# First loads in three DMAs, and three matmul units more beside the last division: one edit of a tuned attention and GLU kernel

## The chip, the cores and the metric

The kernel runs on one core of a Trainium2 chip. The metric is device time in microseconds (us) of one execution. TensorE is called PE in the profile (PEld is its weight load), VectorE DVE, ScalarE ACT, GpSimd POOL and SyncE SP. SP's queue issues most of the DMAs.

## The reference, cut to what matters

```python
x  = A_x                                   # [1, 2048, 512], bf16
xn = (x - mean(x)) / sqrt(var(x) + 1e-5)   # over the 512 columns
# A: 32 heads of 16, causal, window of 256 positions
q, k, v = split(xn @ wqkv)                 # wqkv [512, 1536]
p = softmax(where(0 <= i - j < 256, q @ k.T / 4, -1e9))
a = (p @ v) @ wo                           # wo [512, 512]
# B: gated bilinear layer, F = 1792
b = ((xn @ w_gate) * (xn @ w_up)) @ w_down
out = x + a + b
```

## The kernel before

The 2,048 rows are 16 blocks of 128, and four blocks make a chunk; there are four chunks (T = 0 to 3). All weights are loaded once and stay in SBUF. For each chunk the normalized rows are transposed (`xnT`), projected to Q, K and V (`proj_qk`, `proj_v`), scored, exponentiated and masked strip by strip (`scores`, `mask_diag`), multiplied with V (`values`), divided by the softmax sums (`divide`, which leaves `OT`), and projected with Wo. Beside it run the gate and up matmuls, whose product `hT` goes through Wd (`down`) into the same PSUM sums as the Wo product (`wo`). `store` adds x and writes a block out.

The program order is written out by hand; there is no automatic scheduler. `run` walks through the strips of scores and calls `fill`, which places waiting pieces of work from the list of `fillers` between them. Each piece has a cost in units of one matmul of 512 columns, and `fill(upto)` takes pieces in order as long as half a piece still fits. PSUM tiles come from a pool of four buffers (`ps_m`); behind the last scores the score tiles' four banks become `late[0]` to `late[3]`.

At the start, `setup` puts all loads on SP's queue, in order: blocks 0 and 1 of x, half of the V columns of Wqkv (rows 0 to 255), block 2, the other half, block 3, then the K and the Q columns, and after them the gate and up weights and the rest. PE meanwhile multiplies an identity matrix 38 times (L92). `first_chunk` then takes blocks 0 to 3 through statistics (`norm_stats`, DVE), `norm_scale` (1/sqrt, mostly POOL), `norm_apply` (DVE, gives `xn`), transposes on PE into a PSUM tile `xTp` (L187), a copy by ACT into `xnT` (L189), and the V projection (`vp`, L202). Block 0's four transposes go into one PSUM tile and are copied in two halves. DVE's order is statistics of block 0, of block 1, apply 0, statistics 2, apply 1, statistics 3, apply 2, apply 3. PE's order is transposes 0, transposes 1, V of block 0, transposes 2, V of 1, transposes 3, V of 2, V of 3, then the first K and Q projections (`qkp`, L214). In what follows V0 to V3 are these V projections.

At the end, once the last `values` is done, DVE transposes and divides (L324 to L338) and PE goes on with fillers: `fill(spent + 12)`. Ten matmuls of `down` for block 2 and three of `wo` for block 2 (the head groups 0 to 2) are placed there. Then come the last head group's `wo` for blocks 0 to 2 with their stores, the remaining fillers (`down` of block 3 in two column halves, since its sum is split between `late[3]` and a tile `psd3`), `add_x` for the second half, `wo` of block 3, and two stores: DVE and SP for the first half, ACT for the second.

Of the kernel before, what the change touches and what calls it, by code (L numbers as in the profile page):

```python
# [7 lines left out]
BF16 = mybir.dt.bfloat16  # L8
F32 = mybir.dt.float32
I32 = mybir.dt.int32  # L10
ACT = mybir.ActivationFunctionType
# [14 lines left out]
class Kernel:  # L26
# [26 lines left out]
    def setup(self):  # L53
        nc, const, NT, NF = self.nc, self.const, self.NT, self.NF
        self.x = const.tile([128, NT, 512], BF16, name="x")
        self.Wqkv = const.tile([128, 4, 1536], BF16, name="Wqkv")
        self.Wo = const.tile([128, 4, 512], BF16, name="Wo")
        self.Wg = const.tile([128, 4, self.F], BF16, name="Wg")
        self.Wu = const.tile([128, 4, self.F], BF16, name="Wu")
        self.Wd = const.tile([128, NF, 512], BF16, name="Wd")  # L60
        xv = self.x_d.rearrange("(t p) d -> p t d", p=128)
        wq = self.w_d["qkv"].rearrange("(k p) n -> p k n", p=128)
        wg = self.w_d["g"].rearrange("(k p) n -> p k n", p=128)
        wu = self.w_d["u"].rearrange("(k p) n -> p k n", p=128)
        for b in range(4):
            nc.sync.dma_start(out=self.x[:, b:b + 1, :], in_=xv[:, b:b + 1, :])
            if b in (1, 2):
                ks = slice(2 * b - 2, 2 * b)
                nc.sync.dma_start(out=self.Wqkv[:, ks, 1024:1536], in_=wq[:, ks, 1024:1536])
        for lo in (512, 0):  # L70
            nc.sync.dma_start(out=self.Wqkv[:, :, lo:lo + 512], in_=wq[:, :, lo:lo + 512])
        h = self.F // 2
        for lo in (0, h):
            nc.sync.dma_start(out=self.Wg[:, :, lo:lo + h], in_=wg[:, :, lo:lo + h])
            nc.sync.dma_start(out=self.Wu[:, :, lo:lo + h], in_=wu[:, :, lo:lo + h])
            if lo == 0:
                nc.sync.dma_start(out=self.x[:, 4:8, :], in_=xv[:, 4:8, :])
        nc.sync.dma_start(out=self.Wd[:], in_=self.w_d["d"].rearrange("(f p) n -> p f n", p=128))
        nc.sync.dma_start(out=self.Wo[:], in_=self.w_d["o"].rearrange("(c p) n -> p c n", p=128))
        nc.sync.dma_start(out=self.x[:, 8:NT, :], in_=xv[:, 8:NT, :])  # L80

        warm = const.tile([128, 1], F32, name="warm")
        nc.vector.memset(warm[:], 0.0)
        nc.scalar.activation(out=warm[:], in_=warm[:], func=ACT.Exp)
        ident = const.tile([128, 128], BF16, name="ident")
        nc.gpsimd.memset(ident[:], 0.0)
        nc.gpsimd.affine_select(out=ident[:], in_=ident[:], compare_op=ALU.not_equal, fill=1.0,
                                base=0, pattern=[[-1, 128]], channel_multiplier=1)
        self.ident = ident
        wps = self.ps_m.tile([128, 128], F32, tag="M", name="wps")  # L90
        for _ in range(38):
            nc.tensor.matmul(wps[:], lhsT=ident[:], rhs=ident[:], start=True, stop=True)  # L92
        pi = const.tile([128, 1], I32, name="pi")
        nc.gpsimd.iota(pi[:], pattern=[[0, 1]], base=0, channel_multiplier=1)
        podd = const.tile([128, 1], I32, name="podd")
        nc.vector.tensor_scalar(out=podd[:], in0=pi[:], scalar1=4, scalar2=1,
                                op0=ALU.arith_shift_right, op1=ALU.bitwise_and)
        self.odd = const.tile([128, 1], F32, name="odd")
        nc.vector.tensor_copy(out=self.odd[:], in_=podd[:])
        self.mhalf = const.tile([128, 4], F32, name="mhalf")  # L100
        nc.gpsimd.memset(self.mhalf[:], -0.5)
        self.diag = const.tile([128, 64], BF16, name="diag")
        self.far = const.tile([128, 64], BF16, name="far")
        nc.gpsimd.memset(self.diag[:], BIG)
        nc.gpsimd.memset(self.far[:], BIG)
        for half in (slice(0, 64), slice(64, 128)):
            self.triangle(self.diag[half], True)
            self.triangle(self.far[half], False)
        self.xnT, self.Q, self.hT, self.O, self.OT = {}, {}, {}, {}, {}
        self.K, self.Ko, self.V, self.VS = {}, {}, {}, {}  # L110
        self.strips, self.at = {}, {}
# [63 lines left out]
    def norm_transpose(self, t, by_dma):  # L175

        nc = self.nc
        xn = self.xns.pop(t)
        T, b = divmod(t, 4)
        if b == 0:  # L180
            self.xnT[T] = self.chunk2.tile([128, 4, 4, 128], BF16, tag="xnT", name=f"xnT{T}")
        if by_dma:
            nc.sync.dma_start_transpose(out=self.xnT[T][:, b, :, :], in_=xn[:])
            return
        ps = self.ps_m.tile([128, 4, 128], BF16, tag="M", name="xTp")
        for k in range(4):
            nc.tensor.transpose(ps[:, k, :], xn[:, 128 * k:128 * k + 128], self.ident[:])  # L187
        for ks in (slice(0, 2), slice(2, 4)) if b == 0 else (slice(0, 4),):
            nc.scalar.activation(out=self.xnT[T][:, b, ks, :], in_=ps[:, ks, :], func=ACT.Copy)  # L189

    def bank(self, ks, name):

# [174 lines left out]
    def down(self, T, b, lo, hi):  # L367

        nc = self.nc
        if lo == 0:  # L370
            if T == self.NCH - 1 and b == 3:
                last = self.ps_m.tile([128, 256], F32, tag="M", name="psd3")
                self.sums[b] = [(self.late[3][:, 0:256], 0, 256), (last[:], 256, 512)]
            elif T == self.NCH - 1 and b == 2:
                self.sums[b] = [(self.late[2][:], 0, 512)]
            else:
                self.sums[b] = [(self.ps_m.tile([128, 512], F32, tag="M", name="psd")[:], 0, 512)]
        for f in range(lo, hi):
            for ps, c0, c1 in self.sums[b]:
                nc.tensor.matmul(ps, lhsT=self.hT[T][:, f, 128 * b:128 * b + 128],  # L380
                                 rhs=self.Wd[:, f, c0:c1], start=(f == 0), stop=False)
# [26 lines left out]
    def fillers(self):  # L408
# [54 lines left out]
        for T in range(NCH):  # L463
            if T:
                if T + 1 < NCH:
                    for i, fs in norms(T + 1, 0, 1).items():
                        self.beside[self.first[T, 0] + (0, 2, 3, 4, 5)[i]] = fs
                down(T - 1, 0)
                wo(T - 1, 0, (0, 1))
                for b in range(4):  # L470
                    if b < 3:
                        down(T - 1, b + 1, range(0, NF - 2, 2))
                    wo(T - 1, b, (2, 3))
                    add(0, lambda T=T, b=b: self.store(T - 1, b))
                    if b < 3:
                        down(T - 1, b + 1, range(NF - 2, NF, 2))
                        wo(T - 1, b + 1, (0, 1))
            gu(T, norms(1, 1, 3) if T == 0 else {})
            if T + 1 < NCH:
                project(T + 1)  # L480
# [9 lines left out]
    def run(self):  # L490
# [18 lines left out]
        spent, n, scored = 0, 0, 0  # L509
        valued, ready = -1, -1  # L510

        def fill(upto, group):
            nonlocal spent, n
            while n < len(work):
                cost, f, before, after = work[n]
                if after is not None and after > valued:
                    break
                if spent + cost / 2 > upto and not any(
                        w[2] is not None and w[2] <= group for w in work[n:]):
                    break  # L520
                self.act_free = spent + cost - scored >= ACT_FREE
                f()
                spent += cost
                n += 1
# [29 lines left out]
        T = NCH - 1  # L554
# [7 lines left out]
        spent += VALUES  # L562
        divide(len(steps) - 1)
        valued = ready
        fill(spent + 12, -1)
        for b in range(3):
            self.wo(T, b, (3,))
            self.store(T, b, on_act=(b == 1))
# [42 lines left out]
```

## Time and profile before

| | us |
|---|---|
| median of 4 runs | 270.5 |
| lowest and highest run | 270.32, 271.99 |
| profiled execution, whole | 271.99 |
| its span, first to last instruction | 270.3 |
| PE busy in the span | 260.0 (96%) |
| DVE busy | 181.5 (67%) |
| ACT busy | 170.8 (63%) |
| POOL busy | 113.6 (42%) |

Busy PE time is modelled from pipelined matmuls whose records overlap by their latency, so it is an upper bound of PE's own work. The share of an engine is an average over the span; the prediction reads it by stretch. The profile also shows the clock that TensorE was granted, as a share of its full clock: 0.994 on average over this span.

### The profile page before, as it was taken

To read this page: it belongs to the slowest core of one execution; us is meant where nothing else is said; L and a number is where in the kernel's file an instruction comes from. 1 tells how busy PE (TensorE), PEld (TensorE's weight loads), DVE (VectorE), ACT (ScalarE), POOL (GpSimd) and SP (SyncE) were. 2 spreads that over 40 slices of the span, in tenths; PEclk is the share of its full clock that TensorE was granted. 3 is DMA by queue.
4 is the path that set the end of the run, shared out by engine and by line. 5 is a ranking of instruction groups with operands and counts; after the bars stand their busy time and mean duration, and the time that the engine had idled before them with its cause. 6 is when DMAs were issued, how large, how long until landed. Compare 5 with 4: busy or idle time off the path is not lost.

```text
span 270.3 us, 8862 instructions
## 1 busy us (share of the span) xinstructions
PE 260.0 (96%) x3860; PEld 120.8 (45%) x3882; DVE 181.5 (67%) x352; ACT 170.8 (63%) x132; POOL 113.6 (42%) x281
## 2 busy tenths in 40 slices
PE   7799999999999999999999999999999999999994
PEld 6344444444444444444444444444444444444453
DVE  5267898959656958685675778857752575978260
ACT  3456676597755766769655676768865666665500
POOL 6113242522475344445556443535444354443400
PEclk9799999999999999999999999999999999999999
DMA  5999911110023000001013100000200010000002
GB/s 151 367 373 328 283 24 22 21 43 5 4 61 80 19 2 2 4 2 44 5 19 81 50 11 5 0 4 2 44 5 19 25 39 2 2 0 6 0 2 80
DMA packets 19384, 15.13 MB, mean 56 GB/s; under 512 B 7184, under 2 KB 19344, under 8 KB 19344
## 3 DMA queue, kind: packets, MB, share of 16 engines
q1 hardware_dynamic: 18512, 14.06, 17.9%
q8 instruction: 30, 0.49, 0.8%
q10 hardware_dynamic: 832, 0.49, 0.7%
q14 instruction: 10, 0.08, 0.1%
HBM read 9.70 MB, written 2.10 MB: 44 GB/s over the span
## 4 chain that ended last, share of the span: by engine, by line
PE 86%; DVE 7%; DMA 2%; issue 1%; ACT 1%; SPq 1%; POOL 0%; DVEq 0%; POOLq 0%
PE up L361 17%; PE gp L347 17%; PE psd L380 16%; PE qkp L214 10%; PE S L263 9%; PE acc L318 6%; PE psd L386 5%; PE vp L202 4%; DMA x<-in_A_x_dram 2%; DVE at L324 1%; DVE hT L365 1%; DVE gsb L355 1%; PE L L380 1%; DVE st L151 1%; ACT P L270 1%
## 5 line engine op out<-in xcount | busy, mean ns | idle before, releaser
L270 ACT ACTIVATE P<-S 128x2048 bf16<-128x2048 f32 x76 | 141.0, 1855 | 57.4 <-PE S L263 49.9
L140 POOL TENSOR_SCALAR_AFFINE_SELECT P<-P 64x256 bf16<-64x256 bf16 x224 | 97.2, 434 | 130.3 <-ACT P L270 119.6
L347 PE MATMUL gp<-xnT,Wg 128*128 128x512 bf16 x224 | 60.0, 380 | 0.0
L361 PE MATMUL up<-xnT,Wu 128*128 128x512 bf16 x224 | 59.6, 380 | 0.0
L380 PE MATMUL psd<-Wd,hT 128*128 128x512 bf16 (+1 forms) x198 | 48.8, 372 | 1.4 <-issue 1.3
L365 DVE TENSOR_TENSOR hT<-up,gsb 128x512 bf16<-128x512 f32 x56 | 38.4, 685 | 16.0 <-PE up L361 14.4
L291 DVE TENSOR_TENSOR P<-P,diag 128x512 bf16<-128x512 bf16 (+1 forms) x76 | 30.8, 406 | 10.4 <-ACT P L270 10.4
L380 PEld LDWEIGHTS <-hT 128*128 128x128 bf16 x238 | 22.1, 98 | 24.6 <-issue 2.5
L324 DVE STREAM_TRANSPOSE at<-acc 128x512 f32<-128x512 f32 x30 | 19.7, 695 | 19.8 <-PE acc L318 19.8
L361 PEld LDWEIGHTS <-Wu 128*128 128x128 bf16 x224 | 20.4, 98 | 25.3 <-issue 2.5
L347 PEld LDWEIGHTS <-Wg 128*128 128x128 bf16 x224 | 20.3, 98 | 25.4 <-issue 2.7
L263 PE MATMUL S<-Q,K 16*64 16x320 bf16 (+1 forms) x720 | 31.2, 260 | 0.4
L263 PE MATMUL S<-Q,Ko 32*64 32x320 bf16 (+1 forms) x720 | 31.2, 261 | 0.0
L214 PE MATMUL qkp<-xnT,Wqkv 128*128 128x512 bf16 x128 | 30.0, 380 | 0.0
L263 PEld LDWEIGHTS <-K 16*64 16x64 bf16 x720 | 12.2, 103 | 32.3 <-issue 32.2
L355 DVE CAST gsb<-gp 128x512 bf16<-128x512 f32 x36 | 24.5, 681 | 2.6 <-PE gp L347 1.3
L353 ACT ACTIVATE gsb<-gp 128x512 bf16<-128x512 f32 x20 | 11.9, 597 | 11.8 <-PE gp L347 10.3
L318 PE MATMUL acc<-P,VS 64*32 64x320 bf16 (+4 forms) x672 | 18.9, 254 | 0.0
L318 PE MATMUL acc<-P,V 64*32 64x320 bf16 (+4 forms) x672 | 18.4, 254 | 0.1
L214 PEld LDWEIGHTS <-Wqkv 128*128 128x128 bf16 x128 | 11.7, 98 | 14.5 <-issue 1.4
L202 PE MATMUL vp<-Wqkv,xnT 128*128 128x512 bf16 x60 | 16.4, 404 | 0.5 <-DMA Wqkv<-in_A_wqkv_dram 0.4
L386 PE MATMUL psd<-Wo,OT 128*128 128x512 bf16 (+1 forms) x55 | 15.7, 372 | 1.0 <-issue 0.6
(55 smaller groups left out, 194.6 us busy)
## 6 DMA issues: line engine op xcount, KB each, us to landing
Wg<-in_B_w_gate_dram SPq DMA_DIRECT2D x2, 896.0 KB, 10.6
Wu<-in_B_w_up_dram SPq DMA_DIRECT2D x2, 896.0 KB, 12.8
Wd<-in_B_w_down_dram SPq DMA_DIRECT2D x1, 1792.0 KB, 16.6
out_dram<-y SPq DMA_DIRECT2D x14, 128.0 KB, 1.7
Wqkv<-in_A_wqkv_dram SPq DMA_DIRECT2D x2, 512.0 KB, 7.5
x<-in_A_x_dram SPq DMA_DIRECT2D x1, 1024.0 KB, 11.0
VS<-V SPq DMA_DIRECT2D x6, 144.0 KB, 2.6
x<-in_A_x_dram SPq DMA_DIRECT2D x4, 128.0 KB, 2.6
```

Source lines behind the costliest of these rows:

```text
L140: nc.gpsimd.affine_select(out=v, in_=v, pattern=pattern + [[1 if diag else -1, 64]], compare_op=ALU.is_ge if diag else ALU.is_gt, fill=0.0 ...
L202: nc.tensor.matmul(ps[:], lhsT=self.xnT[T][:, b, k, :], rhs=self.Wqkv[:, k, 1024:1536], start=(k == 0), stop=(k == 3))
L214: nc.tensor.matmul(ps[:], lhsT=self.Wqkv[:, k, lo:lo + 128], rhs=self.xnT[T][:, :, k, :], start=(k == 0), stop=(k == 3))
L263: nc.tensor.matmul(S[64 * par:64 * par + 64, e, col:col + n], lhsT=(self.Ko if par else self.K)[U][rows, c, keys], rhs=self.Q[T][rows, c, ...
L270: nc.scalar.activation(out=P[:, :, 0:col], in_=S[:, :, 0:col], func=ACT.Exp, scale=0.25)
L291: self.nc.vector.tensor_tensor(out=v, in0=v, op=ALU.min, in1=self.diag.unsqueeze(1).unsqueeze(1).to_broadcast([128, 4, n, 64]))
L318: nc.tensor.matmul(accs[par][32 * e:32 * e + 32, q:q + n], lhsT=v, rhs=P[rows, e, col:col + n], start=(i == 0), stop=(i == len(todo) - 1), ...
L347: nc.tensor.matmul(ps[:], lhsT=self.Wg[:, k, 128 * f:128 * f + 128], rhs=self.xnT[T][:, :, k, :], start=(k == 0), stop=(k == 3))
L361: nc.tensor.matmul(ps[:], lhsT=self.Wu[:, k, 128 * f:128 * f + 128], rhs=self.xnT[T][:, :, k, :], start=(k == 0), stop=(k == 3))
L365: nc.vector.tensor_tensor(out=self.hT[T][:, f, :], in0=ps[:], in1=self.gsb[:], op=ALU.mult)
L380: nc.tensor.matmul(ps, lhsT=self.hT[T][:, f, 128 * b:128 * b + 128], rhs=self.Wd[:, f, c0:c1], start=(f == 0), stop=False)
L386: self.nc.tensor.matmul(ps, lhsT=self.OT[T][:, c, 128 * b:128 * b + 128], rhs=self.Wo[:, c, c0:c1], start=False, stop=(c == 3))
```

## The change

Four places change. In `setup` the x blocks 0 to 3 come in two DMAs, block 0 alone and then blocks 1 to 3, and the V columns of Wqkv in one DMA behind them; K and Q follow as before. In `norm_transpose` block 0's four transposes go into two PSUM tiles of two, each copied by ACT as a whole. In `down` the sum of the last block is split in 384 and 128 columns, in place of 256 and 256. And the last `fill` before the final head group has a budget of 15 units instead of 12.

```diff
@@ setup
-        for b in range(4):
-            nc.sync.dma_start(out=self.x[:, b:b + 1, :], in_=xv[:, b:b + 1, :])
-            if b in (1, 2):
-                ks = slice(2 * b - 2, 2 * b)
-                nc.sync.dma_start(out=self.Wqkv[:, ks, 1024:1536], in_=wq[:, ks, 1024:1536])
-        for lo in (512, 0):
+        for lo, hi in ((0, 1), (1, 4)):
+            nc.sync.dma_start(out=self.x[:, lo:hi, :], in_=xv[:, lo:hi, :])
+        for lo in (1024, 512, 0):
             nc.sync.dma_start(out=self.Wqkv[:, :, lo:lo + 512], in_=wq[:, :, lo:lo + 512])
@@ norm_transpose
-        ps = self.ps_m.tile([128, 4, 128], BF16, tag="M", name="xTp")
-        for k in range(4):
-            nc.tensor.transpose(ps[:, k, :], xn[:, 128 * k:128 * k + 128], self.ident[:])
-        for ks in (slice(0, 2), slice(2, 4)) if b == 0 else (slice(0, 4),):
-            nc.scalar.activation(out=self.xnT[T][:, b, ks, :], in_=ps[:, ks, :], func=ACT.Copy)
+        n = 2 if b == 0 else 4
+        for lo in range(0, 4, n):
+            ps = self.ps_m.tile([128, n, 128], BF16, tag="M", name="xTp")
+            for k in range(n):
+                nc.tensor.transpose(ps[:, k, :], xn[:, 128 * (lo + k):128 * (lo + k) + 128], self.ident[:])
+            nc.scalar.activation(out=self.xnT[T][:, b, lo:lo + n, :], in_=ps[:], func=ACT.Copy)
@@ down
-                last = self.ps_m.tile([128, 256], F32, tag="M", name="psd3")
-                self.sums[b] = [(self.late[3][:, 0:256], 0, 256), (last[:], 256, 512)]
+                last = self.ps_m.tile([128, 128], F32, tag="M", name="psd3")
+                self.sums[b] = [(self.late[3][:, 0:384], 0, 384), (last[:], 384, 512)]
@@ run
-        fill(spent + 12, -1)
+        fill(spent + 15, -1)
```

## The prediction

> **What bounds the kernel now.** I read the granted clock first, then busy time by stretch, the chain of waits at both ends, the DMA landings, the timeline of the last 10 us.
>
> Busy time by stretch (start:end, length, then busy us of PE, PEld, DVE, ACT, POOL, granted clock, DMA share, GB/s):
>
> ```profile
> 5.80:9.20 3.40, 1.41 (x10) 0.55 (x9) 1.76 (x6) 1.85 (x4) 1.12 (x4) 1.00 0.91 267
> 9.20:12.60 3.40, 3.29 (x14) 1.74 (x15) 0.47 (x2) 1.54 (x3) 0.70 (x2) 0.50 1.07 388
> 12.60:16.00 3.40, 3.40 (x17) 1.57 (x16) 0.95 (x2) 1.46 (x4) 0.00 (x0) 1.00 1.07 371
> 16.00:66.00 50.00, 49.88 (x688) 21.80 (x687) 41.57 (x82) 35.10 (x29) 18.11 (x43) 1.00 0.45 130
> 252.00:270.30 18.30, 13.99 (x186) 8.09 (x185) 5.12 (x10) 2.86 (x3) 2.50 (x6) 1.00 0.10 30
> ```
>
> From 16 us PE is busy all the time: TensorE bounds the middle, so a microsecond won or lost before 16 us reaches the end. Idle PE is found only before 9.3 us and in the last stretch, and from 9.2 to 12.6 us PE works at half clock. The chain at the start (start, us, what), then, from the DMA view, the issues made at 1.72, 2.70 and 3.18 us (last number: us to landing):
>
> ```profile
> 3.18 4.84 DMA x<-in_A_x_dram
> 8.04 0.70 DVE st L151
> 9.31 0.61 PE xTp L187 x4
> 9.92 1.71 PE vp L202 x4
> 12.05 2.07 PE vp L202 x8
> 14.12 2.59 PE qkp L214 x12
> ```
>
> ```profile
> Wqkv<-in_A_wqkv_dram SPq DMA_DIRECT2D x1, 256.0 KB, 3.2
> Wqkv<-in_A_wqkv_dram SPq DMA_DIRECT2D x1, 256.0 KB, 5.0
> x<-in_A_x_dram SPq DMA_DIRECT2D x1, 128.0 KB, 4.8
> ```
>
> The start waits for block 3 of x: fifth in the queue of loads, landed at 8.0. Its statistics stand in DVE's queue ahead of block 2's normalized rows, so PE has nothing from 8.4 to 9.3. The V weights landed at 4.9 and 7.7. The timeline of the end, and one early row of it (start, us, engine, line):
>
> ```profile
> 6.53 0.40 PE L187 MATMUL xTp<-ident,xn 128*128 128x128 bf16 x4 [0.52 <-DVE xn L171]
> ...
> 260.63 0.81 PE L386 MATMUL L<-Wo,OT 128*128 128x512 bf16 x3
> 261.00 0.71 DVE L338 STREAM_TRANSPOSE OT<-on 128x512 bf16<-128x512 bf16 x1
> 261.77 0.60 PE L386 MATMUL psd<-Wo,OT 128*128 128x512 bf16 x2 [0.32 <-DVE OT L338]
> ...
> 266.23 0.42 DVE L404 TENSOR_TENSOR y<-L,x 128x256 bf16<-128x256 f32 x1 [2.75 <-PE L L386]
> 266.67 0.38 ACT L402 ACTIVATE y<-psd 128x256 bf16<-128x256 f32 x1 [3.66 <-DVE y L404]
> 267.08 0.34 ACTq L405 DMA_DIRECT2D out_dram<-y  x1
> ```
>
> PE runs dry waiting for the last division, works through block 3, and ACT's 64 KB store ends last (2.1 us to landing, 269.2; SP's, issued at 266.68, takes 1.6 and is down at 268.3). ACT's wait is labelled DVE, but in the program its DVE count is met by block 0's store; PE's last matmul releases it.
>
> The profiled execution took 271.99 us: its span of 270.3 and 1.7 around it. It is the slowest of four; the median is 270.5. I sum differences and take them off both.
>
> **Part 1: the loads.** SP issued eight DMAs up to the Q weights, at 0.43 to 0.51 us each; now five. Block 0 is still first (landed 2.9). Blocks 1 to 3 follow at 1.26 as 384 KB, all V weights at 1.72, K at about 2.2 instead of 3.69, Q at 2.7 instead of 4.2. Two landings are not in the trace.
> - L1, blocks 1 to 3. The first 512 KB of before (x0, x1, half of V) were down at 4.92, the last of it issued at 1.72; now issued at 1.26, so 4.5 by that row, 5.5 if the larger piece lags. I take 4.6.
> - L2, all V weights, the 1,024th KB. At the 330 GB/s of 4 to 5 us they need 1.6 us after L1: 6.2. Before, the same 1,024 KB were down at 8.0, after a dip to 80 GB/s between 5.5 and 6.5 us which I can't explain; if it falls worse, 9. I take 7.7, where the second V half landed.
>
> **The new wait.** Block 1's statistics ran at 3.98 because DVE was busy; now they wait for L1. Behind them in DVE's queue stands block 0's xn, which slips from 4.79 to 5.4, with block 0's transposes (5.46 to 6.1), ACT's copies and POOL's rs of block 1. Using before's own distances: xn1 is L1+2.11 (3.98 to 6.09), its transposes +0.44, the first V matmul +0.23: L1+2.78 = 7.4. The cover is L2 at 7.7: 0.3 us. Without it every 0.1 us of L1 costs 0.1. xn2 follows xn1 by 1.30 (as xn1 follows xn0), so block 2's transposes can run at 8.45; xn3, 1.98 after its statistics (8.04 to 10.02), gives block 3's at 9.6. x is no longer the wait; the V weights are, then ACT.
>
> PE from there, at full clock (0.86 per V block of four, 0.25 per four transposes): V0 7.7 to 8.56, transposes, V1 8.8 to 9.66, transposes, V2 to 10.8. ACT, in order at 0.6 each (V0 out, xnT2, V1 out, xnT3), frees V3 only at 11.15: done at 12.0. The same walk for before at full clock (transposes at 9.31 and 10.47, xnT3 at 11.65) ends at 12.5: gain 0.5. With half clock in 9.2 to 12.6, half of V1, the transposes, V2 and one matmul of V3 fall into it, and V3 ends at 13.25, against 13.96 in the trace: gain 0.7. I take 0.6. Weights: K landed at 10.7 and Q at 12.2 with as many KB before them, in time for 12.0 and 12.9. Loads behind are paced by the full queue (SP sat 1.81 us in Wu's issue), so I give them no gain; their users come at 21.8 us and later. The copies of V into VS that ACT issues land at 25.2 and are first used at 32.6.
>
> **The clock, row against rule.** Between 5.8 and 9.2 PE was busy 1.41 of 3.40 us, and the next 3.4 us ran at 0.50. The Trainium skill (TensorE: Matmul & The Clock Gate, "What's actually happening") says that the activity window is free-running, about 3.4 us, half rate after an idle one. By the row alone the halved stretch belongs to both kernels (gain 0.6). By the rule it is drawn anew each execution: the other three runs, 1.4 to 1.7 us shorter, may have escaped it (3.4 us at half clock costs 1.7), though profiling overhead would look the same. In 5.8 to 9.2 the changed kernel has about 2.0 busy us (two sets of transposes, V0, a third set, half of V1). If that keeps the clock where before lost it, the start gains 13.96 − 12.0 = 1.95.
>
> **Part 2: two PSUM tiles.** ACT may copy block 0's first half after two transposes, perhaps 0.2 us sooner. V0 doesn't start before 7.7 and the copies are done by 7.2: nothing; without that cover, 0.2 gained. No instruction is added on PE or ACT, and the program shows no new wait.
>
> **Part 3: the end.** One `down` call of block 3, cost 2, now fits before the last `wo`: in the program four matmuls (two of 384, two of 128 columns), 2 × 512 columns at 0.216 = 0.43 us. PE's last issue slot ends at 261.28 (third `wo` matmul at 261.06 plus 0.216), the division at 261.71: the gap of 0.49 to 261.77 takes them in, 0.06 to spare. All after moves up by 0.43.
> The split costs as many columns. Row: four transposes of 128 columns, each with its weight load, take 0.40 us at full clock, one alone 0.219: 0.060 apiece, and 0.162 + 0.060 = 0.222 per pair, against 0.219 for two of 256. The rule speaks against it (same page, "Back-to-back issue gap": about 81 ns per matmul of 128 columns with its weights): 18 pairs at +0.024 would take back 0.43. I go with the row: nothing.
> ACT's last read falls from 256 to 128 columns: (0.597 − 0.383)/2 = 0.107 less. DVE's part ends 0.21 before PE's end instead of 0.43, and lasts 0.55 for 384 columns (0.42 for 256, 0.69 for 512): it starts at 266.01, SP issues at 266.6, down at 268.2. ACT's store lands at 268.65, still last. Its rows shrink to 256 bytes: by the nearest row (64 KB of 512-byte rows 2.1 us, 128 KB of 1,024-byte rows 2.0) no change, between −0.1 and +0.3. Sum of the end: −0.54.
>
> **Sum.** −0.6 − 0.54 = −1.1 us: 270.9 for an execution like the profiled one, 269.4 as a median.
>
> **The rivals.**
> - The clock stays up where it fell: −1.95 − 0.54 = −2.5: 268.0. For it: 2.0 busy us against 1.41. Against: three runs may have been there already.
> - One part is worth nothing. Start eaten by L1 at 5.4 or L2 at 8.2: −0.5, 270.0. Or weights at 81 ns: −0.7, 269.8.
> - Slower: the V weights in one piece land late and the clock falls with them. Before, V0's first two matmuls needed only the half down at 4.92. From L2 = 8.2 the start gains nothing; from 8.8 the stretch 5.8 to 9.2 holds under 1.1 busy us, and half clock follows even in runs that escaped it. At L2 = 9.0 the chain V0 to V3 ends at 14.6, not 12.5: +2.1 − 0.5 = +1.6: 272.1. For it: the dip, and K and Q queued 1.5 us sooner beside V. Against: they stand behind V in one queue.
>
> **How the numbers follow.** As worked out 50% (own range 268.9 to 269.9), clock kept 22%, one part lost 18%, slower 10%. This kernel's runs tell about 0.5% (1.35 us) from no change: faster means under 269.15, the second case and a third of the first, 0.39; slower means over 271.85, 0.07; the rest 0.54. The range leaves out the slow case and the far end of the clock case: 267.8 to 270.8.
>
> **What would show it.** Right: statistics of block 1 at 4.4 to 5.0 with the idle before them put to DMA x; the first `vp` matmul waiting for DMA Wqkv until 7.4 to 8.0; first `qkp` at 12.0 (clock kept) or 13.25 (not); no idle before the last `wo`; last ACT read near 0.28 us. Wrong: first `vp` after 8.8, 0.50 clock in a longer stretch, pairs in the tail above 0.23 us, or the last store over 2.4 us.

## The result, and the profile after

The changed kernel takes 268.91 us (median of 36 executions), the kernel before 270.57 (57 executions). The ratio is 0.9944, 95% interval 0.9931 to 0.9957: 1.5 us less, between 1.2 and 1.9. The ratio is that of the means; the medians lie 1.66 us apart. The prediction had said 1.1 less.

The two profiled executions lie further apart, with spans of 270.3 and 267.1 us: 3.2 us. The one of before is one of the longer of its kernel (271.99 against a median of 270.57), the one of after is typical (268.90). Two readings have to be kept apart from here on: what the change did to these two executions, and what it did to most.

Busy time by stretch in the profile after (columns as before: PE, PEld, DVE, ACT, POOL, granted clock, DMA share, GB/s):

```profile
5.80:9.20 3.40, 2.48 (x19) 1.22 (x20) 2.57 (x7) 2.18 (x5) 2.41 (x5) 1.00 1.05 360
9.20:12.60 3.40, 3.40 (x19) 1.53 (x19) 0.14 (x2) 2.44 (x5) 0.00 (x0) 1.00 1.06 382
```

In this execution the stretch of half clock from 9.2 us is gone, and between 5.8 and 9.2 the loads run at 360 GB/s where they ran at 267. The chain at the start, and the landings of blocks 1 to 3 and of the V weights, issued at 1.25 and 1.72 us:

```profile
1.25 3.19 DMA x<-in_A_x_dram
4.46 0.70 DVE st L148
...
5.67 0.61 DVE st L148
...
6.86 0.61 DVE st L148
...
8.09 0.40 PE xTp L186 x4
8.49 0.86 PE vp L200 x4
9.35 0.31 PE xTp L186 x4
9.66 1.90 PE vp L200 x8
11.57 2.59 PE qkp L212 x12
```

```profile
x<-in_A_x_dram SPq DMA_DIRECT2D x1, 384.0 KB, 3.2
Wqkv<-in_A_wqkv_dram SPq DMA_DIRECT2D x1, 512.0 KB, 4.3
```

The wait is now for the 384 KB of blocks 1 to 3, until 4.44. From there DVE takes the statistics of blocks 1 to 3 without a further wait for a load, and PE follows it. The V weights are down at 6.0, a microsecond before their first use at 7.15. The first `qkp` runs 2.55 us earlier than in the profile before (14.12 to 11.57 in the chain). The end:

```profile
258.12 0.81 PE L384 MATMUL L<-Wo,OT 128*128 128x512 bf16 x3
258.49 0.71 DVE L336 STREAM_TRANSPOSE OT<-on 128x512 bf16<-128x512 bf16 x1
258.77 0.33 PE L378 MATMUL L<-Wd,hT 128*128 128x384 bf16 x1
258.93 0.22 PE L378 MATMUL psd<-Wd,hT 128*128 128x128 bf16 x1
258.99 0.33 PE L378 MATMUL L<-Wd,hT 128*128 128x384 bf16 x1
259.15 0.22 PE L378 MATMUL psd<-Wd,hT 128*128 128x128 bf16 x1
259.26 0.61 PE L384 MATMUL psd<-Wo,OT 128*128 128x512 bf16 x2
...
263.44 0.56 DVE L402 TENSOR_TENSOR y<-L,x 128x384 bf16<-128x384 f32 x1 [2.47 <-PE L L384]
263.66 0.28 ACT L400 ACTIVATE y<-psd 128x128 bf16<-128x128 f32 x1 [3.17 <-PE psd L384]
263.97 0.36 ACTq L403 DMA_DIRECT2D out_dram<-y  x1
```

The four added matmuls stand in the gap, and the last `wo` no longer shows a wait on PE. Matmul pairs of 384 and 128 columns start 0.22 us apart (258.77 to 258.99). SP's store is issued at 264.03, just behind ACT's, and lands last (2.1 us, at 266.1; ACT's 32 KB take 1.7).

### The profile page after: what moved, and what is told of

Its sections match the earlier page's. It is cut to its first block, busy times and chain, and to the rows that moved or that the text cites. A ratio compares the mean times of both kernels' runs of the same rounds, so it can differ in the third digit from the quotient of the medians.

```text
span 267.1 us, 8861 instructions
## 1 busy us (share of the span) xinstructions
PE 257.9 (97%) x3860; PEld 118.8 (44%) x3882; DVE 181.7 (68%) x352; ACT 170.6 (64%) x132; POOL 113.8 (43%) x281
## 4 chain that ended last, share of the span: by engine, by line
PE 88%; DVE 7%; issue 1%; DMA 1%; ACT 1%; SPq 0%; POOL 0%; DVEq 0%; POOLq 0%
PE up L359 17%; PE gp L345 17%; PE psd L378 16%; PE qkp L212 11%; PE S L261 9%; PE acc L316 6%; PE psd L384 5%; PE vp L200 4%; PE L L378 2%; DVE hT L363 1%; DMA x<-in_A_x_dram 1%; DVE st L148 1%; DVE at L322 1%; DVE gsb L353 1%; DVE xn L168 1%
## 5 line engine op out<-in xcount | busy, mean ns | idle before, releaser
L261 PEld LDWEIGHTS <-K 16*64 16x64 bf16 x720 | 12.2, 103 | 32.3 <-issue 32.2
L316 PEld LDWEIGHTS <-V 64*32 64x32 bf16 x720 | 14.6, 90 | 2.8 <-issue 2.4
## 6 DMA issues: line engine op xcount, KB each, us to landing
Wu<-in_B_w_up_dram SPq DMA_DIRECT2D x2, 896.0 KB, 12.5
```

Of the source, the lines that this page charges most:

```text
L261: nc.tensor.matmul(S[64 * par:64 * par + 64, e, col:col + n], lhsT=(self.Ko if par else self.K)[U][rows, c, keys], rhs=self.Q[T][rows, c, ...
L316: nc.tensor.matmul(accs[par][32 * e:32 * e + 32, q:q + n], lhsT=v, rhs=P[rows, e, col:col + n], start=(i == 0), stop=(i == len(todo) - 1), ...
```

## The experiments

Each run is set beside executions of the kernel before on the same chip. The start of the first `qkp` is taken from PE's timeline (13.96 before, 11.40 after). Medians in us:

| | edit | this | before | first `qkp` |
|---|---|---|---|---|
| e1 | loads only | 269.95 | 270.44 | 11.72 |
| e2 | two PSUM tiles only | 270.48 | 270.44 | 11.78 |
| e3 | budget only | 270.07 | 270.44 | 12.54 |
| e4 | split only | 270.04 | 270.44 | 12.23 |
| e12 | budget and split | 269.66 | 270.39 | 12.22 |
| e5 | loads, V in halves | 270.12 | 270.47 | half clock |
| e6 | loads, x in four | 269.73 | 270.47 | 11.20 |
| e7 | changed kernel, x in 1, 1, 2 | 268.48 | 270.47 | 11.01 |
| e8 | changed kernel, ten more identity matmuls | 269.09 | 270.47 | 11.34 |
| e9 | changed kernel, warm-up of 28 | 270.06 | 270.39 | 11.48 |
| e10 | changed kernel, warm-up of 48 | 269.04 | 270.39 | 11.47 |
| e11 | e7 with six more identity matmuls | 268.56 | 270.39 | 11.36 |

### The parts one by one: e1 to e4 and e12

e1 takes the `setup` hunk of the diff alone, e2 the `norm_transpose` hunk, e3 the last hunk, e4 the `down` hunk, e12 the last two together.

> Only the five loads in place of eight; transposes, tail split and budget as before. Theory 1 (the early landing of blocks 1 to 3 and of all V weights is most of the gain, about 1.1 us in an execution whose clock stays up): 269.4 us, ratio 0.996, first vp matmul near 7.2 us. Theory 2 (the start is worth 0.6 as predicted, the tail more than predicted): 269.9 us. Theory 3 (the loads gain only because PE's clock no longer falls): 268.8 us or less, like the whole change.

> Only block 0's transposes in two PSUM tiles. Hidden behind block 1's transposes and the V weights: no change, 270.5 us. Rival: the earlier first copy lets V0 start sooner, 0.2 us less, 270.3.

> Only the budget of 15 units in place of 12; the last block's sum stays split 256 to 256. The four matmuls fit into the 0.49 us in which PE waits for the division: 0.43 us less, 270.1 us. Rival: the wait for the division ends later or the last stores take over, so that nothing or less than 0.2 us remains.

> Only the split of 384 to 128 columns, with the budget of 12. By the 0.060 us that a 128-column matmul took in the transposes: pairs at 0.22 us, ACT's last read 0.28 instead of 0.38, about 0.1 us less or no change. Rival (81 ns per matmul of 128 columns): pairs at 0.24, 0.3 us more.

> Both edits of the end (budget of 15, split of 384 to 128), loads and transposes as before. By the prediction's sum 0.54 us less: 269.9. If the shorter landing of the last stores seen with the split alone (2.0 us where 256 to 256 took 2.1 to 2.4) is real, 0.7 to 0.8 less: 269.7. If the two overlap: 0.4 less.

By medians the loads give 0.5 us. By the ratio this is not told from zero (0.9993, interval 0.9975 to 1.001), because seven of e1's 21 usual executions lie at 271.32 to 271.92 and the rest at 269.56 to 270.36 (on this, see the half clock below). The PSUM tiles give nothing, the budget 0.4 (0.9991, 0.9975 to 1.0007), the split 0.4 (0.9984, 0.9972 to 0.9997), the two edits of the end together 0.7 (0.9967, 0.9949 to 0.9984). The profiles say more than the times, because the middle of the kernel is rigid: from the first `qkp` to the first `at<-L` transpose of the end it takes 244.57 to 244.63 us in every profile named here, before, after and e1 to e4 and e12 alike. So start and end can be read separately.

Start. e2, e3, e4 and e12 have the old loads, and none of them shows the half clock of the profile before. Their chain in e2:

```profile
3.19 3.99 DMA x<-in_A_x_dram
7.20 0.70 DVE st L151
8.47 0.40 PE xTp L189 x4
8.86 0.86 PE vp L203 x4
10.04 1.90 PE vp L203 x8
11.94 2.59 PE qkp L215 x12
```

V0 to V3 take 0.86 us per block here, as after the change; in the profile before they took 1.71. Block 3 lands at 7.2 here, at 7.6 to 7.9 in e3, e4 and e12, at 8.0 before: it varies by 0.8 us between executions, and the first `qkp` with it. In e2, e3, e4 and e12 the first `qkp` starts 4.58 us after the statistics of block 3 (these at 7.20, 7.96, 7.65 and 7.64). With the new loads it starts 6.94 or 6.95 us after the statistics of block 1 (after, e1, e8, e9, e10: 4.46, 4.78, 4.40, 4.53, 4.52). So the landing that each kernel waits for sets its start, and what follows takes the same time in each execution.

With the old loads the first `qkp` starts at 12.19 on average (e2, e3, e4, e12), with the new ones at 11.48 (after, e1, e8, e9, e10): 0.71 us. This is what the loads are worth in most executions. Theory 1 of e1 put it at 1.1 and theory 2 at 0.6; it is nearer to the second. Theory 3 falls: e1's profile keeps a full clock and is far from 268.8. The times of e2, 270.48 against 270.44 (ratio 0.9996, interval 0.9983 to 1.001), could hide a gain of 0.2 from the PSUM tiles, but the distances leave no room for it: 4.58 us with two tiles (e2) and with one (e3, e4, e12), and with the new loads 6.94 with two (after) and with one (e1).

End. From the first `at<-L` transpose to the landing of the last store: 10.67, 10.74 and 10.96 us with the old end (before, e1, e2), 10.47 in e3, 10.44 in e4, 10.07 in after and 10.06 in e12. So both edits give 0.72 on average. Of this, 0.53 is that the last store is issued sooner (8.54 us after that transpose with the old end, 8.01 in after); the rest is a shorter landing. The medians agree: e12's 269.66 is what its second line expected (269.7). In e3 the last DVE read starts 7.25 us after that transpose instead of 7.69: the 0.43 of the added matmuls and nothing else. In e4:

```profile
264.70 0.56 DVE L404 TENSOR_TENSOR y<-L,x 128x384 bf16<-128x384 f32 x1 [2.91 <-PE L L386]
264.93 0.28 ACT L402 ACTIVATE y<-psd 128x128 bf16<-128x128 f32 x1 [3.60 <-PE psd L386]
265.23 0.36 ACTq L405 DMA_DIRECT2D out_dram<-y  x1
```

ACT's read is 0.10 shorter, and DVE and ACT finish together, so both stores go out within 0.06 us. The last of them lands 2.0 to 2.1 us after its issue; with the old split ACT's store, issued 0.4 us behind SP's, took 2.1 (before), 2.2 (e1 and e6), 2.4 (e2 and e3) and 2.6 (e5). That is how e4 gains more than the 0.1 us expected. Why the landing is shorter, size or spacing, was not separated.

0.71 and 0.72 make 1.4 of the 1.5 us (1.2 to 1.9) measured.

### What in the loads did it: e5, e6 and e7

```diff
 # e5, on the kernel before: blocks 1 to 3 grouped, V still in halves
+        for lo, hi in ((0, 1), (1, 4)):                   # x
+        for ks in (slice(0, 2), slice(2, 4)):             # V columns
 # e6, on the kernel before: x in four, then V in one
+        for lo, hi in ((0, 1), (1, 2), (2, 3), (3, 4)):   # x
+        for lo in (1024, 512, 0):                         # V, K, Q
 # e7, on the changed kernel
-        for lo, hi in ((0, 1), (1, 4)):
+        for lo, hi in ((0, 1), (1, 2), (2, 4)):
```

> The loads of the change, but the V weights in two halves behind the x blocks (six DMAs); all else as before. If bringing blocks 1 to 3 ahead of the V weights is what gains: the same as the three-DMA start alone, 269.8 us in its full-clock executions, first vp matmul at 7.2 to 7.5 us. If one large V DMA matters by itself: 0.3 us or more slower than that, with the second half down later than 6.3 us.

> Blocks 0 to 3 of x as four DMAs ahead of all V weights in one; all else as before. If only the order matters, block 1's statistics run at 4.0 instead of 4.5 to 4.8 and all four blocks are down by 5: the chain to the first qkp becomes shorter by up to 0.5 us, 269.4 us. If single blocks lag for being small (the fourth landed at 7.2 to 8.0 before), no better than before, 270.4 us.

> The changed kernel with x in three DMAs (block 0, block 1, blocks 2 and 3) in place of two. The chain after is DVE's: block 1's statistics wait for the 384 KB until 4.46. With block 1 alone they start at 4.0: first vp at 6.7, first qkp at 10.9 to 11.0, 268.4 us. Rival: the V weights then are the wait (down at 6.0 to 6.3 plus one more issue of 0.5 us ahead of them), and less than 0.2 us remains.

By the traces the order of the DMAs decides, not their number or size. In e6 four single blocks ahead of V are all down by 4.4 us (2.1 to 2.2 us after their issue), though they are as small as before. The loads in the stretch from 5 to 7 us, first in the profile before, then in e6 (the last number is GB/s):

```profile
5.00:7.00 2.00, 1.48 (x17) 1.18 (x15) 1.35 (x4) 0.70 (x3) 1.49 (x4) 1.00 0.64 144
```

```profile
5.00:7.00 2.00, 1.48 (x15) 1.10 (x13) 1.93 (x6) 0.83 (x3) 1.67 (x4) 1.00 1.04 359
```

The same stretch has 187 to 232 GB/s in the four other profiles with x and V interleaved, 304 in e5, 329 and 343 in after and e1. So the slow stretch comes with x and V pieces in turn and goes with x first. Why interleaving slows them was not found. e6 also shows the wait that the prediction had put first, because V is issued at 2.68 there:

```profile
7.04 1.02 PE L199 MATMUL vp<-Wqkv,xnT 128*128 128x512 bf16 x4 [0.24 <-DMA Wqkv<-in_A_wqkv_dram]
```

V lands 4.3 us after its issue, at 7.0, and costs 0.24 us. In the change V is issued at 1.72 and is out of the way. e5's profile happened to be an execution at half clock (below), so its first `qkp` can't be compared. What stands before it can: block 1's statistics start at 4.46 and the transposes of blocks 0 and 1 at 5.73 and 6.92, as after the change, and the V halves are down at 5.4 and 6.4, before V0 at 7.32. Its other times, 269.84 to 270.29, are some 0.3 us above e1's lower group, as its second theory had it. The start of its profile shows no cost of the halves, but the last store takes 2.6 us to land, 0.4 more than in e1. Whether that is so in its other executions is not known, so a cost of the halves isn't fully excluded.

e7 goes after the wait that the change brought in. With block 1 in a DMA of its own its statistics run at 4.01 instead of 4.46, and the first `qkp` at 11.01: 0.39 earlier than after the change, as its first theory said. 268.48 us, ratio to before 0.9926 (0.9906 to 0.9946), the lowest median of all.

### The half clock: e8 to e11

```diff
 # e8 (ten) and e11 (six, with the loads of e7), behind norm_transpose(0, False)
+        for _ in range(10):
+            self.nc.tensor.matmul(self.wps[:], lhsT=self.ident[:], rhs=self.ident[:], start=True, stop=True)
 # e9 (28) and e10 (48)
-        for _ in range(38):
+        for _ in range(28):
```

The times of the changed kernel fall into two groups: 28 of 36 between 268.72 and 269.25, eight between 270.37 and 270.84 (the text of e8 says nine). There are two kinds of slower execution. In one the clock drops, as in the profile before: of the 146 executions of the kernel before that stand beside e1 to e12, 13 took 271.83 to 272.90 us, and they alone show a mean granted clock of 0.994 or less. Two of the eight slower executions of the changed kernel show 0.994 too. The other six show 1.00, and so do five of e1's seven. e5's profile caught this other kind in its own kernel (span 270.0, granted clock 1.00). Its PE timeline, then the granted clock of the same time:

```profile
1.43 4.23 PE L91 MATMUL wps<-ident 128*128 128x128 bf16 x38 [1.43 <-POOL ident L86]
5.73 0.61 PE L186 MATMUL xTp<-ident,xn 128*128 128x128 bf16 x4
6.92 0.61 PE L186 MATMUL xTp<-ident,xn 128*128 128x128 bf16 x4 [0.58 <-DVE xn L170]
7.32 1.91 PE L201 MATMUL vp<-Wqkv,xnT 128*128 128x512 bf16 x4
```

```profile
5.80:9.20 3.40, 2.82 (x14) 1.46 (x15) 2.56 (x7) 1.26 (x3) 2.42 (x5) 1.00 1.02 348
```

V0 lasts 1.91 us where four matmuls at full clock last 1.03, and the transposes 0.61 instead of 0.40: PE has not come up from the pace of its first matmuls (0.107 us apart in the warm-up, in all profiles), and gets there only in V1. The granted clock reads 1.00 all the while, because the trace holds no record of it before 10.49 us and the view prints 1.00 where there is none. It shows the drop in the profile before, but not a clock that has not yet risen; the pace of the matmuls is the better witness. In the profile after, the record begins at 4.59 us, and there the warm-up matmuls go from 0.107 to 0.056 us apart.

> The changed kernel with ten more identity matmuls of 128 columns behind block 0's transposes, where PE waits 0.8 us for block 1 anyway. If the second cluster of times of the changed kernel (270.4 to 270.8 us, 9 of 36, against 268.9 for the others) is PE at half clock for one 3.4 us stretch after too little work, it disappears or gets rarer, and the median stays at 268.9. If it is something else (a late load), its share stays at about a quarter.

> The changed kernel with 28 identity matmuls at the start in place of 38, so that PE falls idle at 4.4 instead of 5.2 to 5.7 us. If the second cluster is PE staying at half clock until about 10.7 us because its warm-up filled no whole 3.4 us stretch, most executions now fall into it: median about 270.6, and the profile shows first V matmuls 0.43 us apart. If it has another cause: median 268.9, a quarter at 270.7.

> The changed kernel with 48 identity matmuls in place of 38 (busy until 5.8 at full clock, 6.6 at half). If the second cluster comes from the warm-up, it disappears; the median stays within 0.1 us of 268.9, since block 1's transposes only run at 6.9. If not, a quarter stays at 270.7.

> x in DMAs of one, one and two blocks, and six more identity matmuls behind block 0's transposes (they end by 6.5 even at half clock, where block 1's transposes start). The version expected to be best: median 268.5, like the one without the six, and no execution above 269.5.

With 28 warm-up matmuls nine of twelve executions lie at 269.97 or above (median 270.06) and three at 268.90 to 268.99; with 38, eight of 36 lie above 270; with 48, none of seven; with the ten extra ones of e8, none of six. A shorter warm-up makes the slower group larger, so the warm-up is at least part of its cause; e9's profile caught one of its three fast executions, so the late clock itself was not seen there. That more matmuls make the group vanish isn't shown: the groups of six and seven are small, and e7 without any extra matmuls had none in six either. e11 is no better than e7 (268.56 against 268.48), and its profile speaks against a simple cure: PE is busy without a break from 1.43 us on, yet its clock comes up only at 7.43, behind V0's first matmul, and the first `qkp` runs 0.35 us later than in e7.

## Why the prediction was right, step by step

- **The bound.** Right: TensorE carries a shift at the start unchanged through the middle, to within 0.06 us.
- **L1.** Right: 4.44 against 4.6. The new wait is there, behind it xn0 at 5.29 (5.4 predicted), block 0's transposes at 5.73 (6.1), block 1's at 6.91, the first V matmul at 7.15: L1+2.71, predicted L1+2.78.
- **L2.** Mis-sized: 6.0 against 7.7, just under the lower bound of 6.2. The step that failed is taking the slow stretch of before as a property of the first megabyte; e5 and e6 show that it belongs to the interleaved order. K and Q, put at 10.7 and 12.2 by the pace of before, were down at 8.1 and 9.6. The price was small, because the second claim failed with it: not the V weights but DVE's chain of blocks is the wait, and it lets V0 start at 7.15 instead of 7.7. The cover for L1 that the V weights were to give does not exist, which is why e7 still gains 0.4.
- **The walk to the first `qkp`.** V3 was to end at 12.0; the first `qkp` runs at 11.40, and 0.55 of the 0.6 is V0's earlier start. With the old loads at full clock it runs at 12.19, predicted 12.5: block 3 landed at 7.6 on average there, and the prediction had taken the 8.0 of one profile. The gain is 0.71, predicted 0.5, or 0.6 with the half clock weighed in. That the two errors, 0.6 and 0.3, have the same sign and partly cancel is luck.
- **The clock.** The reading by the rule fitted better than the reading by the single row. e2, e3, e4 and e12 kept the old loads and full clock, so the stretch of the profile before was not the usual case; e3 was busy for only 1.26 us between 5.8 and 9.2, less than the 1.41 before, and did not fall. The Trainium skill (TensorE: Matmul & The Clock Gate, "What's actually happening") gives a free-running window of about 3.4 us, and the record of the clock before agrees with the length: it changes at 5.79, 9.20 and 12.61. The changed kernel was busy for 2.48 us in that stretch, more than the 2.0 predicted, but whether this keeps the clock up was not tested: two of its 36 executions still show 0.994. The profiled pair did what the rival "the clock stays up" said and more, 2.55 us at the start where it had 1.95, but the medians did not.
- **PSUM tiles.** Right at nothing, but not for the reason given: the V weights, down at 6.0, covered nothing. The first V matmul came behind block 1's transposes.
- **The end.** The four matmuls took the gap, 0.43 to 0.44 us. The 81 ns of the Trainium skill (same page, "Back-to-back issue gap") for a 128-column matmul with its weights is not seen: pairs of 384 and 128 start 0.22 us apart, as the row said. ACT's read is 0.10 shorter. Wrong was who lands last: SP's store, not ACT's, and the estimate that the landing would not change; the last store was issued 0.53 sooner, and with the shorter landing the end gained 0.72 where 0.54 was predicted. ACT's store of 32 KB in rows of 256 bytes took 1.7 us; whether the short rows cost anything can't be read from it, since its size changed too.
- **The sum.** 0.71 + 0.72 in place of 0.6 + 0.54; both terms were a little small and no sign was wrong.

## What to carry to other kernels

When a first load is waited for, put the inputs of the first chain ahead of all weights, and check in the trace which transfer is really last; grouping them matters less than the order, and a group is waited for as a whole. A gap on the busiest engine of a tail is filled one for one by work that has to be done anyway. One profiled execution may be of the rarer kind: compare its time with the median before its stretches are taken as the kernel's.

## What the runs showed of the hardware

- Interleaved loads of x rows and V weight columns ran at 144 to 232 GB/s between 5 and 7 us, and x first and then V at 304 to 359, with the same bytes.
- A PE that has not yet reached its full clock is not seen in the granted clock of the profile: 1.00 beside V matmuls that took 634 ns each, against 379 at full clock (e5). The record of the clock begins where it comes up: between 4.6 and 6.7 us in twelve of the fourteen profiles, at 7.4 in e11 and at 10.5 in e5, though the first matmul ran at 1.4 in each.
- Of two stores issued almost together, ACT's 32 KB in rows of 256 bytes landed after 1.7 us, SP's 96 KB after 2.0 to 2.1; 64 KB issued 0.4 us behind another 64 KB took 2.1 to 2.6.
